# Long convolution by FFT and soft mixture of experts on one core: narrower first-stage products, a last stage packed into row groups, and an in-place spectral product

## The chip, the cores and the metric

The kernel runs on one core of a Trainium2 chip. The metric is the device time in microseconds of one execution, lower is better; the time given is the median of three runs. The engines are called by the profile's names: PE (matrix products; PEld is its weight load), DVE and POOL (elementwise), ACT (elementwise, and the copies out of PSUM), SP (issues nearly all transfers). PSUM is the memory that PE writes; it has eight banks of 128 x 512 floats.

## The reference

```python
def _attn_ref(x, h):                 # x: (8, 5696, 128), h: (5696, 128)
    Xf = np.fft.rfft(x, n=2 * S, axis=1); Hf = np.fft.rfft(h, n=2 * S, axis=0)
    return np.fft.irfft(Xf * Hf[None], n=2 * S, axis=1)[:, :S, :]

def _moe_ref(x, phi, w1, w2):        # x: (45568, 128), phi: (128, 32), 8 experts, 4 slots each
    logits = x @ phi
    d = exp(logits - logits.max(0)); d /= d.sum(0) + 1e-9
    slot_input = (d.T @ x).reshape(E, S_per_e, D)
    slot_out[e] = np.maximum(slot_input[e] @ w1[e], 0.0) @ w2[e]
    c = exp(logits - logits.max(1)); c /= c.sum(1) + 1e-9
    return c @ slot_out
```

Every channel of eight sequences is convolved with a filter of the same length. The result, seen as 45568 tokens, goes through a soft mixture of experts: one softmax over all tokens (dispatch), one over the 32 slots (combine).

## The kernel before

All data is float32, and each matrix product shows as two MATMUL passes in the profile. The convolution is a transform of length 90 x 64 in two stages, written as matrix products, with a product of spectra between and two stages back. There are nine groups: the filter (g = 0) and the eight sequences. Between the stages the data goes through buffers in DRAM: `f` behind the first stage, `z` behind the third.

**Stage A** (first stage, 90 frequencies). `load_x` (L190) loads a chunk of four columns n2 and their four mirror columns: 89 rows of 2 KB runs, in two transfers of 80 and 9 partitions. `fold` (L201, on POOL) makes the sum (comp 0) or the difference (comp 1) of the two halves. `stage_a(c, comp)` multiplies it (L212) by two tables of 128 columns, ACT copies each bank out (L214), and two transfers of 45 partitions, in runs of 1 KB, store to `f` (L218). A group has eight chunks.

**Stage B** works on units of four pairs of frequencies, twelve to a group. `load_g` (L236) loads `gt` from `f`; `stage_b1` makes the second transform (L250) into the two-bank PSUM tile `bt`, multiplies it by the filter's spectrum (L270, DVE, two products `pr` and `pi` in SBUF) and adds (L279, DVE; in the steps below 27 and from 72 on one of the two adds is POOL's). For the filter's group the products are with `turn`, and the sums (L274) are Hr and Hi. `stage_b2` is the third transform (L294); ACT copies the result out (L299), and one transfer of 512 KB stores it to `z` (L302).

**Stage C** works on pairs T, four to a sequence. `load_pair` (L330) loads 64 and 26 partitions of 16 KB runs. `stage_c1` makes the last transform: four products of 90 frequencies (128 rows with zeros), each as two column halves (L349); ACT copies two of the banks to `y` (L358) and `om` (L362); `fold_out` (L354, L355, DVE) forms sums and differences with the other two; four operations on POOL (L368) mirror them. Then `stage_c2` transposes (L377), `stage_c3` makes the logits (L386), `stage_c4` transposes them (L415), takes the row maximum (L430, DVE) and subtracts it (L431, POOL), `stage_c5` transposes the exponentials (L438), `softmax` ends the combine weights (L451 on POOL), `dispatch` accumulates the slots (L462), `stage_c6` transposes the combine weights (L486) and stores them. At the end come the experts and the output products (L819).

The order is written out by hand in one loop over steps t, and each engine runs its instructions in that order. Each step below 72 has one chunk of stage A; units of stage B come one (odd t) or two (even t) to a step; from t = 27 on `stage_c1` runs in every odd step. So two steps make a cycle. The core of the step, shortened:

```python
stage_a(t, 0); fold(t + 1, 0)
dispatch(pair(3)); slot_b(1)                # even steps
after = stage_c1(T, rows)                   # odd steps; rows is stage_c4
stage_c2(pair(1)); stage_c6(pair(5))        # even steps
after()                                     # odd steps: fold_out of om, four L368
slot_b(2); load_pair(pair(-2)); load_x(t + 3); stage_c5(U)
stage_a(t, 1); fold(t + 1, 1)
stage_c3(pair(1)); slot_b(3)                # even steps
```

`slot_b` makes `stage_b1` of one unit and `stage_b2` of the unit before. Each `fold` has one buffer to a comp. The products of stages A and C take their PSUM banks in turn from a ring of four until the end of stage B, then of eight.

Of the kernel before, what the change touches and what calls it, by code (L numbers as in the profile page):

```python
# [10 lines left out]
F32 = mybir.dt.float32  # L11
AF = mybir.ActivationFunctionType
AL = mybir.AluOpType
# [4 lines left out]
def z_blocks(n):  # L18

    return [(0, 64, 32), (64, n - 64, 0)]  # L20


def transform_tables(S, N1, N2, CH, X0, F0, F1):

# [14 lines left out]
    s1 = np.stack([np.cos(a1), -np.sin(a1), -np.cos(a1)], 1)  # L41
    a0 = np.outer(alpha, np.arange(N1 // 2) + 0.5)
    i1 = np.stack([np.cos(a0), -np.sin(a0), -np.cos(a0)], 1)
    NP = N1 // 2
    part = s1
    s1 = np.zeros((P, 3, P))
    for a, p in enumerate((F0, F1)):
        s1[X0:X0 + R1, :, p:p + NP] = part[:, :, a * NP:(a + 1) * NP]
    part = i1[np.arange(N1).reshape(2, NP).T.reshape(-1)]
    i1 = np.zeros((P, 3, N2))  # L50
    for r, n, p in z_blocks(N1):
        i1[p:p + n, :, 0:NP] = part[r:r + n]
# [5 lines left out]
    back = np.arange(N2).reshape(2, HALF // CH, CH).transpose(1, 0, 2).reshape(-1)  # L58
# [5 lines left out]
    for a in range(2):  # L64
        wq[a] = w[a * NP:(a + 1) * NP].transpose(1, 0, 2)
        for q in range(NP):
            vq[q % 2, :, q // 2, a] = w[a * NP + q][back].T
            tn[q % 2, :, 0, q // 4, a, q // 2 % 2] = np.cos(turn[a * NP + q]) / N
            tn[q % 2, :, 1, q // 4, a, q // 2 % 2] = np.sin(turn[a * NP + q]) / N
    wq, vq, tn = [t.reshape(P, *t.shape[2:]) for t in (wq, vq, tn)]  # L70
    return [np.ascontiguousarray(t, dtype=np.float32) for t in (s1, i1, wq, vq, tn)]
# [3 lines left out]
def kernel(  # L75
# [42 lines left out]
    assert S == R1 * N2 and R1 == N1 - 1 and D == P and CH == Q == 4  # L118
    SPLIT = R1 // 16 * 16
    X0, F0, F1 = 20, 6, 82  # L120
    ctx.enter_context(tc.manual_schedule())

    t_s1, t_i1, t_w, t_v, t_turn = [
        nc.inline_tensor(t, f"tab_{n}").ap()
        for n, t in zip(("s1", "i1", "w", "v", "turn"), transform_tables(S, N1, N2, CH, X0, F0, F1))]
    fd = [nc.dram_tensor(f"f_{g}", (2, N2, NP, 2, D), F32, kind="Internal").ap() for g in range(B + 1)]
    zd = [nc.dram_tensor(f"z_{b}", (NP, 2 * N2, 2, D), F32, kind="Internal").ap() for b in range(B)]
# [8 lines left out]
    i1 = const.tile([P, 3, HP], F32, name="i1")  # L136
# [24 lines left out]
    s1 = apool.tile([P, 3, P], F32, name="s1", tag="s1", bufs=1)  # L161
# [12 lines left out]
    xf = [apool.tile([P, CH, D], F32, name=f"x{i}", tag=f"x{i}", bufs=1) for i in range(2)]  # L174
# [4 lines left out]
    def load_x(c):  # L179
        if c >= (B + 1) * NJ:  # L180
            return
        g, j = divmod(c, NJ)
        src = (h if g == 0 else x[g - 1]).rearrange("(a n) d -> a n d", n=N2)
        t_ = xcs[c % len(xcs)]
        gap = N2 - CH * (2 * j + 1)
        for r in (slice(0, SPLIT), slice(SPLIT, R1)):
            v = src[r, CH * j:CH * (j + 1), :]
            v = bass.AP(tensor=v.tensor, offset=v.offset,
                        ap=[v.ap[0], [gap * D, 2], [1, CH * D]])
            nc.sync.dma_start(  # L190
                out=t_[X0 + r.start:X0 + r.stop, :, :, :].rearrange("p s n d -> p s (n d)"), in_=v)
        xs[c] = t_
# [3 lines left out]
    def fold(c, comp):  # L196
# [3 lines left out]
        y_ = xf[comp]  # L200
        nc.gpsimd.tensor_tensor(out=y_[:, :, :], in0=t_[:, 0, :, :], in1=t_[:, 1, ::-1, :],  # L201
                                op=AL.subtract if comp else AL.add)
        folded[(c, comp)] = y_

    def stage_a(c, comp):
        g, j = divmod(c, NJ)
        src = folded.pop((c, comp))
        tab = (0, 1) if comp == 0 else (1, 2)
        st = apool.tile([P, CH, 2, D], F32, name="fst", tag="fst", bufs=5)
        for G in range(2):  # L210
            p = bank()
            nc.tensor.matmul(p[:, :], s1[:, tab[G], :],  # L212
                             src[:, :, :].rearrange("p n d -> p (n d)"), start=True, stop=True)
            nc.scalar.activation(st[:, :, G, :],  # L214
                                 p[:, :].rearrange("p (n d) -> p n d", d=D), AF.Copy)
        n0 = comp * HALF + CH * j
        for a, p in enumerate((F0, F1)):
            nc.sync.dma_start(  # L218
                out=fd[g][a, n0:n0 + CH, :, :, :].rearrange("n q c d -> q n (c d)"),
                in_=st[p:p + NP, :, :, :].rearrange("k n c d -> k n (c d)"))  # L220
# [9 lines left out]
    def load_g(u):  # L230
        if u >= (B + 1) * NW:
# [5 lines left out]
            out=t_[:, 0:n, :, :].rearrange("p q c d -> p (q c d)"),  # L237
            in_=fd[g].rearrange("a r q c d -> (a r) (q c d)")[:, 8 * w * D:(8 * w + 2 * n) * D])
        gs[u] = t_

    def stage_b1(u, share):
# [15 lines left out]
        else:  # L257
            pv = bt[r, :, 0, :].rearrange("p a (c d) -> p a c d", c=2)
        k = 2 * m
        tags = ("yf", "yf") if g == 0 and w % 2 else ("pr", "pi")  # L260
        pr, pi = [bpool.tile([P, 4, 2, D], F32, name="p", tag=x, bufs=2 if x == "yf" else 1)
                  for x in tags]
        for p_, H_ in ((pr, turn[:, 0]), (pi, turn[:, 1])) if g == 0 else ((pr, Hr), (pi, Hi)):
# [6 lines left out]
            nc.vector.tensor_tensor(out=p_[r, 0:k, :, :], in0=pv, in1=h_, op=AL.mult)  # L270
        if g == 0:
            for c, op_, H_, eng in ((0, AL.add, Hr, nc.vector), (1, AL.subtract, Hi, nc.gpsimd)):
                h_ = H_[r, w, :, :, :].rearrange("p a o d -> p (a o) d") if m == 2 else H_[r, w, :, 0, :]
                eng.tensor_tensor(out=h_, in0=pr[r, 0:k, c, :], in1=pi[r, 0:k, 1 - c, :], op=op_)  # L274
            return
        y_ = bpool.tile([P, 4, 2, D], F32, name="yf", tag="yf", bufs=2)
        for c, op_, eng in ((1, AL.add, nc.gpsimd if share else nc.vector),
                            (0, AL.subtract, nc.vector)):
            eng.tensor_tensor(out=y_[r, 0:k, c, :], in0=pr[r, 0:k, c, :],  # L279
                              in1=pi[r, 0:k, 1 - c, :], op=op_)  # L280
        prods[u] = y_

    def stage_b2(u):
# [6 lines left out]
        for o, (i, n) in enumerate(us):  # L290
# [11 lines left out]
        nc.sync.dma_start(  # L302
            out=zd[g - 1][4 * w:4 * w + k, :, :, :].rearrange("q r c d -> r q (c d)"),
            in_=st[:, :, :, :].rearrange("p o q x -> p (o q) x")[:, 0:k, :])
# [4 lines left out]
    zn = used = None  # L309
    ybufs = [ypool.tile([P, Q * CH, D + 1], F32, name=f"y{i}") for i in range(2)]  # L310
    zring = [ypool.tile([P, 2, 2, CH, 2, D], F32, name="zc")]
# [4 lines left out]
    nc.vector.memset(zring[0][:, :, :, :, :, :], 0.0)  # L316
# [5 lines left out]
    def load_pair(T):  # L322
# [5 lines left out]
        w_ = 2 * 2 * CH * 2 * D  # L328
        for r, n, p in z_blocks(N1):
            nc.sync.dma_start(  # L330
                out=t_[p:p + n, :, :, :, :, :].rearrange("k h o n c d -> k (h o n c d)"),
                in_=zd[b].rearrange("q (a r) c d -> (q a) (r c d)",
                                    a=2)[r:r + n, j * w_:(j + 1) * w_])
        zs[T] = t_

    def stage_c1(T, between):
        t_ = zs.pop(T)
        kr = used if t_ is zn else P
# [7 lines left out]
        def product(o, tab, q):  # L346
            p = bank()
            for h_ in range(2):
                nc.tensor.matmul(p[h_ * HP:(h_ + 1) * HP, :], i1[0:kr, tab, :],  # L349
                                 t_[0:kr, h_, o, :, q, :], start=True, stop=True)  # L350
            return p[:, :].rearrange("p (n d) -> p n d", d=D)

# [4 lines left out]
        b_, a_ = product(0, 1, 1), product(0, 0, 0)  # L357
        nc.scalar.activation(part(0, 0), b_, AF.Copy)  # L358
        fold_out(a_, part(0, 0), part(1, 0))
# [506 lines left out]
```

## Time and profile before

| | |
|---|---|
| median of three runs | 924.53 us (923.91 to 933.71) |
| span of the profiled execution | 922.1 us; the page gives no other time for it |
| PE, PEld | 818.0 us (89%), 423.9 us (46%) |
| DVE, ACT, POOL | 653.1 us (71%), 481.7 us (52%), 488.1 us (53%) |
| moved by DMA | 272.45 MB, mean 295 GB/s, 156552 packets |
| largest groups | L212 on PE 275.9 us, L201 on POOL 192.8 us, L214 on ACT 171.9 us |
| f stores, gt loads, z stores, z loads | 288, 108, 96 and 64 transfers |

The page describes one profiled execution. "Busy" is the time in which an engine ran instructions of its own; matmuls are pipelined, so a busy PE need not be at its peak. The line of tenths shows the busy share in 40 equal slices of the span. In a timeline each line is a run of like instructions: start, length, engine, source line, operation, output and input, count, and in brackets the idle time before it and what ended it. SPq is SP's queue.

### The profile page before, as it was taken

To read this page: it belongs to the slowest core of one execution; us is meant where nothing else is said; L and a number is where in the kernel's file an instruction comes from. 1 tells how busy PE (TensorE), PEld (TensorE's weight loads), DVE (VectorE), ACT (ScalarE), POOL (GpSimd) and SP (SyncE) were. 2 spreads that over 40 slices of the span, in tenths; PEclk is the share of its full clock that TensorE was granted. 3 is DMA by queue.
4 is the path that set the end of the run, shared out by engine and by line. 5 is a ranking of instruction groups with operands and counts; after the bars stand their busy time and mean duration, and the time that the engine had idled before them with its cause. 6 is when DMAs were issued, how large, how long until landed. Compare 5 with 4: busy or idle time off the path is not lost.

```text
span 922.1 us, 19325 instructions
## 1 busy us (share of the span) xinstructions
PE 818.0 (89%) x7220; PEld 423.9 (46%) x7220; DVE 653.1 (71%) x887; ACT 481.7 (52%) x888; POOL 488.1 (53%) x426
## 2 busy tenths in 40 slices
PE   6968898899999999999999999999987777878893
PEld 2323344345444445544554454444444434345783
DVE  3047665478888878888888788988887775674552
ACT  4623454455556655555666666656553344475442
POOL 4648766546655565556565655655466552472000
PEclk9989999899999999999999999999999888798865
DMA  9989999999899999999999999999989887761798
GB/s 298 279 274 299 272 345 311 289 345 327 268 320 319 314 282 324 316 314 285 341 304 327 289 324 329 297 318 320 316 269 330 272 254 198 211 249 73 272 405 341
DMA packets 156552, 272.45 MB, mean 295 GB/s; under 512 B 11766, under 2 KB 114422, under 8 KB 153317
## 3 DMA queue, kind: packets, MB, share of 16 engines
q1 hardware_dynamic: 155883, 270.85, 91.4%
q8 instruction: 58, 0.95, 0.4%
q10 hardware_dynamic: 576, 0.36, 0.2%
q14 instruction: 35, 0.29, 0.1%
HBM read 142.86 MB, written 128.21 MB: 294 GB/s over the span
## 4 chain that ended last, share of the span: by engine, by line
PE 51%; DMA 31%; POOL 5%; DVE 5%; issue 3%; SPq 2%; ACT 2%; DVEq 0%; POOLq 0%; ACTq 0%
PE bank L212 17%; DMA zc<-z 11%; PE bank L349 9%; DMA gt<-f 8%; PE bt L250 7%; PE bz L294 6%; DMA out_dram<-o 4%; PE bank L377 4%; DVE p L270 2%; POOL y L368 2%; DMA f<-fst 2%; PE bank L462 2%; DMA z<-zst 2%; PE bank L438 2%; PE bank L386 2%
## 5 line engine op out<-in xcount | busy, mean ns | idle before, releaser
L212 PE MATMUL bank<-x,s 128*128 128x512 f32 x576 | 275.9, 614 | 12.3 <-POOL x L201 12.0
L201 POOL TENSOR_TENSOR x<-xc 128x512 f32<-128x512 f32 x144 | 192.8, 1342 | 154.7 <-PE bank L212 70.4
L214 ACT ACTIVATE fst<-bank 128x512 f32<-128x512 f32 x288 | 171.9, 597 | 95.5 <-PE bank L212 74.8
L299 ACT ACTIVATE zst<-bz 128x1024 f32<-128x1024 f32 x96 | 93.2, 971 | 205.4 <-PE bz L294 198.5
L270 DVE TENSOR_TENSOR p<-bt,Hr 128x1024 f32<-128x1024 f32 x96 | 112.9, 1176 | 108.0 <-PE bt L250 95.7
L212 PEld LDWEIGHTS bank<-x,s 128*128 128x128 f32 x576 | 102.4, 193 | 131.5 <-issue 93.4
L279 DVE TENSOR_TENSOR yf<-p 128x512 f32<-128x512 f32 (+1 forms) x163 | 146.4, 931 | 3.3
L250 PE MATMUL bt<-gt,wt 64*64 64x256 f32 x1620 | 116.4, 394 | 25.1 <-DMA gt<-f 22.0
L349 PE MATMUL bank<-zc,i 128*64 128x512 f32 x480 | 117.1, 610 | 7.0 <-DMA zc<-z 4.1
L294 PE MATMUL bz<-yf,vt 64*64 64x256 f32 x1440 | 104.9, 393 | 15.5 <-POOL yf L279 15.0
L270 DVE TENSOR_TENSOR p<-bt,Hi 128x1024 f32<-128x1024 f32 x96 | 112.3, 1170 | 0.0
L250 PEld LDWEIGHTS bt<-gt,wt 64*64 64x64 f32 x1620 | 55.0, 134 | 102.0 <-issue 31.6
L368 POOL TENSOR_TENSOR y<-y,op 128x512 f32<-128x512 f32 x64 | 77.5, 1211 | 7.8 <-DVE op L354 5.1
L294 PEld LDWEIGHTS bz<-yf,vt 64*64 64x64 f32 x1440 | 58.2, 137 | 44.2 <-POOL yf L279 21.0
L279 POOL TENSOR_TENSOR yf<-p 128x512 f32<-128x512 f32 (+1 forms) x29 | 45.9, 1583 | 53.9 <-DVE p L270 53.9
L368 POOL TENSOR_TENSOR y<-y,om 128x512 f32<-128x512 f32 x54 | 71.8, 1330 | 2.1
L270 DVE TENSOR_TENSOR p<-bt,turn 128x1024 f32<-128x1024 f32 (+1 forms) x24 | 27.2, 1174 | 57.8 <-PE bt L250 57.7
L349 PEld LDWEIGHTS bank<-zc,i 128*64 128x64 f32 x480 | 30.8, 138 | 68.3 <-issue 40.8
L377 PE MATMUL bank<-ident,y 109*128 109x109 f32 x512 | 60.0, 275 | 0.7 <-DVE y L368 0.7
L377 PEld LDWEIGHTS bank<-ident,y 109*128 109x128 f32 x512 | 53.5, 151 | 13.6 <-issue 11.9
L379 ACT ACTIVATE yt<-bank 128x360 f32<-128x360 f32 x128 | 50.9, 482 | 3.3 <-PE bank L377 3.3
L819 PE MATMUL op<-so,cT 32*128 32x128 f32 x704 | 46.0, 374 | 4.4 <-ACT o L828 3.6
(97 smaller groups left out, 851.5 us busy)
## 6 DMA issues: line engine op xcount, KB each, us to landing
f<-fst SPq DMA_DIRECT2D x288, 180.0 KB
gt<-f SPq DMA_DIRECT2D x99, 512.0 KB
z<-zst SPq DMA_DIRECT2D x88, 512.0 KB
zc<-z SPq DMA_DIRECT2D x30, 1024.0 KB
xc<-in_x_dram SPq DMA_DIRECT2D x64, 320.0 KB
out_dram<-o SPq DMA_DIRECT2D x16, 1024.0 KB
zc<-z SPq DMA_DIRECT2D x30, 416.0 KB
out_dram<-o SPq DMA_DIRECT2D x8, 768.0 KB
```

What stands on the lines that cost most here:

```text
L201: nc.gpsimd.tensor_tensor(out=y_[:, :, :], in0=t_[:, 0, :, :], in1=t_[:, 1, ::-1, :], op=AL.subtract if comp else AL.add)
L212: nc.tensor.matmul(p[:, :], s1[:, tab[G], :], src[:, :, :].rearrange("p n d -> p (n d)"), start=True, stop=True)
L214: nc.scalar.activation(st[:, :, G, :], p[:, :].rearrange("p (n d) -> p n d", d=D), AF.Copy)
L250: nc.tensor.matmul(bt[q * HP:(q + 1) * HP, a, o, :], wt[r, 2 * i + q, :], t_[r, 2 * o + q, :, :].rearrange("p c d -> p (c d)"), start=True ...
L270: nc.vector.tensor_tensor(out=p_[r, 0:k, :, :], in0=pv, in1=h_, op=AL.mult)
L279: eng.tensor_tensor(out=y_[r, 0:k, c, :], in0=pr[r, 0:k, c, :], in1=pi[r, 0:k, 1 - c, :], op=op_)
L294: nc.tensor.matmul(bz[a * HP:(a + 1) * HP, q, o, :], vt[r, i, a, :], y_[r, a * m + o, :, :].rearrange("p c d -> p (c d)"), start=True, sto ...
L299: nc.scalar.activation(st[:, 0:m, 0:n, :].rearrange("p o q x -> p q o x"), bz[:, 0:n, 0:m, :], AF.Copy)
L349: nc.tensor.matmul(p[h_ * HP:(h_ + 1) * HP, :], i1[0:kr, tab, :], t_[0:kr, h_, o, :, q, :], start=True, stop=True)
L368: eng.tensor_tensor(out=part_, in0=part(v, 0), in1=o_[:, :, :], op=sign)
L377: nc.tensor.transpose(p[:, i * TR:(i + 1) * TR], ys[T][0:TR, k * CH + i, 0:D], ident[0:TR, 0:TR])
L379: nc.scalar.activation(yt[:, k * CH:(k + 1) * CH, :, :], of_tokens(p), AF.Copy)
```

## The change

Tables and layouts change with the stages; what is computed stays.

- Stage A: the 90 frequencies are split into columns of 60 and 30. `stage_a(t, False)` makes the 60 of a chunk from both comps at once, two products of 64 columns side by side in one bank. `stage_a(t, True)`, in odd steps, makes the 30 of the last two chunks, four products of 32 columns side by side. Each stored run is 4 KB. The two folds of a chunk have one of three buffers of their own. The last nine rows of x go to partitions 100, 103, ... 124.
- Stage B: `gt` is loaded in runs of 1 KB. `pi` is made first; the other product overwrites `bt` in PSUM, and the adds read `bt` and `pi`. All adds are DVE's.
- `z` is stored by part of n2, in four transfers of 32 partitions (frequencies below 64), or eight (the last four units). C1's loads take two transfers of 128 partitions. Rows of the second buffer that no store fills are set to zero once, by eight transfers on ACT's queue.
- C1: 64 frequencies of both parts side by side in two row groups, and the other 26 in four row groups of 32, accumulated in the same four banks, which are all taken before `stage_c4`.

```diff
-        y_ = xf[comp]
+        y_ = xf[c % len(xf)]
...
-    def stage_a(c, comp):
+    def stage_a(c, high):
...
+        if high:
+            groups = [(c_, o, HALF, slice(HP, HP + HALF)) for c_ in (c - 1, c) for o in range(2)]
+        else:
+            groups = [(c, o, HP, slice(0, HP)) for o in range(2)]
+        for q in range(2):
             p = bank()
-            nc.tensor.matmul(p[:, :], s1[:, tab[G], :],
-                             src[:, :, :].rearrange("p n d -> p (n d)"), start=True, stop=True)
+            for i, (c_, o, m, cols) in enumerate(groups):
+                nc.tensor.matmul(p[i * m:(i + 1) * m, :], s1[:, q + o, cols], columns(c_, o),
+                                 start=True, stop=True)
...
-        for p_, H_ in ((pr, turn[:, 0]), (pi, turn[:, 1])) if g == 0 else ((pr, Hr), (pi, Hi)):
+        for p_, H_ in (((pi[r, 0:k, :, :], turn[:, 1]), (pv, turn[:, 0])) if g == 0 else
+                       ((pi[r, 0:k, :, :], Hi), (pv, Hr))):
...
-        for c, op_, eng in ((1, AL.add, nc.gpsimd if share else nc.vector),
-                            (0, AL.subtract, nc.vector)):
-            eng.tensor_tensor(out=y_[r, 0:k, c, :], in0=pr[r, 0:k, c, :],
-                              in1=pi[r, 0:k, 1 - c, :], op=op_)
+        for c, op_ in ((1, AL.add), (0, AL.subtract)):
+            nc.vector.tensor_tensor(out=y_[r, 0:k, c, :], in0=pv[:, :, c, :],
+                                    in1=pi[r, 0:k, 1 - c, :], op=op_)
...
-        b_, a_ = product(0, 1, 1), product(0, 0, 0)
-        nc.scalar.activation(part(0, 0), b_, AF.Copy)
-        fold_out(a_, part(0, 0), part(1, 0))
+        ps = {(o, c): bank() for o, c in ((0, 1), (1, 0), (0, 0), (1, 1))}
+        for c in (1, 0):
+            for h_ in range(2):
+                for o in range(2):
+                    r = slice(o * HP, (o + 1) * HP)
+                    nc.tensor.matmul(ps[o, c][h_ * HP:(h_ + 1) * HP, :], im[r, c, :],
+                                     zt[r, h_, :, c, :], start=True, stop=False)
+        for h_ in range(2):
+            for (o, c), p in ps.items():
+                r = slice((2 * o + c) * HALF, (2 * o + c) * HALF + N1 - MAIN)
+                nc.tensor.matmul(p[h_ * HP:(h_ + 1) * HP, :], ir[r, :], zx[r, h_, :, :],
+                                 start=False, stop=True)
+        nc.scalar.activation(part(0, 0), ps[0, 1], AF.Copy)
+        nc.scalar.activation(om[:, :, :], ps[1, 0], AF.Copy)
+        fold_out(ps[0, 0], part(0, 0), part(1, 0))
+        a_ = ps[1, 1]
         between()
-        b_, a_ = product(1, 1, 0), product(1, 2, 1)
-        nc.scalar.activation(om[:, :, :], b_, AF.Copy)
...
         if t < NA:
-            stage_a(t, 0)
+            stage_a(t, False)
             fold(t + 1, 0)
...
         if t < NA:
-            stage_a(t, 1)
+            if t % 2:
+                stage_a(t, True)
             fold(t + 1, 1)
```

## The prediction

> **What bounds the kernel now.** I read the page first, then stretches of the span, then one cycle of the middle in the order of time, then the waits and the chain that ended last.
>
> ```profile
> PE 818.0 (89%) x7220; PEld 423.9 (46%) x7220; DVE 653.1 (71%) x887; ACT 481.7 (52%) x888; POOL 488.1 (53%) x426
> DMA  9989999999899999999999999999989887761798
> ```
>
> TensorE and the DMA engines are both near full. By stretches, from the first product of stage C1 (182.60) to the last that still has stage A after it (664.70):
>
> ```profile
> 182.60:664.70 482.10, 469.80 (x4146) 234.99 (x4145) 407.14 (x542) 286.70 (x521) 277.02 (x240) 1.00 0.99 313
> ```
>
> The columns are the length, busy PE, PEld, DVE, ACT, POOL, granted clock, DMA share, GB/s. These 482.1 us hold 22 cycles of two steps, 21.91 us each, PE busy 21.35 of them, POOL only 12.6. So PE's order sets the pace and DMA just keeps up. One cycle, from stage A of an odd step on:
>
> ```profile
> 466.11 1.98 PE L212 MATMUL bank<-x,s 128*128 128x512 f32 x4
> ...
> 468.13 0.60 ACT L214 ACTIVATE fst<-bank 128x512 f32<-128x512 f32 x1 [0.26 <-PE bank L212]
> ...
> 468.72 1.94 PE L349 MATMUL bank<-zc,i 128*64 128x512 f32 x8 [0.62 <-ACT fst L214]
> ...
> 470.58 0.66 PE L415 MATMUL bank<-ident,lt 128*128 128x128 f32 x4
> ...
> 471.28 0.60 ACT L419 ACTIVATE L<-bank 128x512 f32<-128x512 f32 x1 [0.85 <-PE bank L415]
> ...
> 472.24 0.68 DVE L430 TENSOR_REDUCE rm<-L 128x16 f32<-128x512 f32 x1
> ...
> 472.36 0.60 ACT L362 ACTIVATE om<-bank 128x512 f32<-128x512 f32 x1
> ...
> 473.04 1.09 PE L250 MATMUL bt<-gt,wt 64*64 64x256 f32 x16
> 473.06 1.05 POOL L431 TENSOR_TENSOR L<-L,rm 128x512 f32<-128x512 f32 x1 [0.47 <-DVE rm L430]
> 473.23 0.69 DVE L354 TENSOR_TENSOR op<-bank,om 128x512 f32<-128x512 f32 x1 [0.31 <-PE bank L349]
> ...
> 474.07 2.44 POOL L368 TENSOR_TENSOR y<-y,op 128x512 f32<-128x512 f32 x2
> ...
> 475.42 3.60 PE L212 MATMUL bank<-x,s 128*128 128x512 f32 x8
> ...
> 476.48 2.76 POOL L368 TENSOR_TENSOR y<-y,om 128x512 f32<-128x512 f32 x2
> ...
> 478.95 1.09 PE L462 MATMUL bank<-y,d 128*32 128x129 f32 x32
> 479.20 1.71 POOL L201 TENSOR_TENSOR x<-xc 128x512 f32<-128x512 f32 x1
> ...
> 483.89 1.95 PE L212 MATMUL bank<-x,s 128*128 128x512 f32 x4
> ```
>
> The reader should follow POOL: after C1 it runs L431, four L368, and only then the second fold (L201) of the next chunk, ready at 480.91. PE began that chunk's first half (the last four of the eight L212) near 477.1 and needs the second fold only at 483.89. So the fold has 3 us to spare today, 3.8 us after the chunk's stage A began.
>
> **The change, part by part.** A matmul is two passes, one per 0.43 us for 512 columns (3.60 for eight); two side by side (L349) take eight passes in 1.94, four side by side (L250, 256 columns) sixteen in 1.09, so packing loses almost nothing.
>
> Stage A: four full products a chunk (3.44 us) become four of 64 columns, two side by side (1.72), and per two chunks eight of 32 columns, four side by side (1.72): 2.58 a chunk, 1.7 us less PE in a cycle. One eviction in four goes: 72 x 0.60 = 43 us of ACT, which is hidden (ACT is at 52%). C1: sixteen passes of 64 rows, four together (1.72), and sixteen of 26 rows, eight together (0.86; 1.72 if only four): 2.58 for 3.44. PE's own work so falls by 2.6 us a cycle.
>
> But stage A's first matmul pair now takes the even and the odd fold together, at the top of the step. In the even step that fold is the one that POOL makes after the four L368. This is a new wait, and behind it on PE stand the dispatch, two units of stage B, C2, C6, C3, stage A of the odd step, and the next C1, which feeds POOL. It closes a loop, and I add it up from E, the end of stage A in the odd step.
>
> C1 now takes four banks at once, and its second matmul needs the bank that stage A has just filled: the eviction ends 0.9 after E (L214: 0.26 wait and 0.60). Then 2.58: 3.45 with the first pass done early. Copy of the first bank 0.65: 4.1. The copy of om 0.60 and the transposes of L415 0.66 run together: 4.75; eviction of L 0.60: 5.35; rm 0.68: 6.05. Op on DVE 0.69: 6.75, while POOL's L431 takes 1.05: 7.15. Four L368 at 1.22: 12.05. Fold 1.27: 13.3. PE has meanwhile done L415, one unit each of B1 and B2, C5, the 32-column products and one 64-column product, and stands from about 9.7, so it idles 3.6 us. The rest of stage A, 1.7: 15.0. From the end of stage A to the next L212 (478.95 to 483.89) PE spends 4.94: 19.95. C3 waits for C2's evictions, 0.55, and takes 0.75; the next unit 1.8; stage A 1.7: 24.75.
>
> So a cycle is 24.75 instead of 21.91: 22 x 2.84 = +62. Low end: no 0.9 wait for the bank, 24.0, +46. High end: the rest of C1 only four side by side (+0.85), and the slow rows of L368 and L201 above (2.76 and 1.71: +0.75), 26.35, +98.
>
> In-place product: the second product is written to PSUM, of which no row exists. Nearest are L270 (1.22, PSUM to SBUF) and twice that. I take 1.22; the adds read PSUM and SBUF, as L354 does at 0.69, in place of L279's 0.98. DVE has 19.0 busy in 22.3 and loses none of its reserve. The bank pair is held 1.4 longer, but the next unit comes 5 us later; without that gap it would cost 1.4 a unit.
>
> DMA: the f stores become runs of 4 KB and the gt loads runs of 1 KB; by the trace's packet records (46 ns for one of 1 KB, 159 for 4 KB) one saves about what the other costs. The z stores go from 96 to 512. Each issue takes 0.32 us at least (L302), so 416 x 0.32 = 133 us more on SP, 4 us of each cycle. SP is issuing 14.5 us in the cycle shown; 18.5 fits into 24.75. The z loads now cover 128 partitions each, for 64 and 26.
>
> A rule of the Trainium skill speaks against this part: "DMA: Bandwidth & Descriptors" (Rules for kernel authors) wants many small transfers joined. With the fixed 2.0 us of that page (Anatomy of one DMA, for another kind of queue) and eight in flight, an estimate from it is 416 x 2.0 / 8 = 104 us, and the sum below would be 1071. The row has 0.32 us of issue, which lies beside the POOL loop, and the sum goes by that.
>
> The idle 3.6 us also touches the clock. In 160 to 168.8 us, where PE was busy 5.72 of 8.80, the granted clock was 0.81; in the middle, where gaps are short, 1.00. The Trainium skill, "TensorE: Matmul & The Clock Gate" (Part 1), halves the clock after a whole idle window of about 3.4 us; an estimate by it is that a gap of 3.6 us covers a window in one cycle of twenty, +2 us in all, and a gap of 5 us in half of them. No row here shows gaps of this size in the middle, and I add nothing.
>
> Before 182.6: PE loses 27 x 0.86 = 23 us of work, but gt loads and x loads end the waits there, and more stores and eight transfers of zeros come in. I take -1; from -12 (the share of L212 in the chain there, a quarter of it) to +10 (half of some 60 extra issues). From 664.7 to 769 the chain shows POOL's share of the yf sums:
>
> ```profile
> 692.90 1.23 POOL yf L279
> 694.17 1.67 PE bz L294 x16
> ```
>
> That goes to DVE. The cycle there is 20.8; DVE's own 17.6 (three units of 2 x 1.22 + 2 x 0.69, and 6.2 of the stages C) and 5.7 MB at about 300 GB/s (19) remain. 5 x 2 = -10, from -16 to 0. The tail waits twice for z loads:
>
> ```profile
> 773.48 11.15 DMA zc<-z
> ```
>
> Spread over all partitions, without the copy of the gap ahead, I take 3.5 off each (11.15 and 10.77) and 1 for C1: -8, from -14 to 0.
>
> **Sum.** +62 - 1 - 10 - 8 = +43 on the span of 922.1, 965. The median of the runs stands 2.4 above the span, so 967.5 us. What a measurement can tell here from no change is about 1%, 9 us.
>
> **Rivals.** Hidden wait: the saving of PE shows after all. Its place is the same loop, E to fold. It decides if the fold is ready by 11.3 instead of 13.3, as a cycle of 22.8 is then paid for by the 19 saved elsewhere; if it ends at DMA's floor, 21.0, the time is 22 x -0.9 - 19 = -39, 885. For it: POOL is at 53%, and its L368 might run faster when DVE no longer adds SBUF to SBUF. Against: five operations in a row, none under 1.05.
>
> SP's queue: its 34 issues a cycle, at the 0.63 mean of the cycle shown (14.5 for 23), are 21.4, and with 5 us of waits that are left, 27 a cycle: +112 - 19, 1018. For it: "SPq L236 <- DMA zc<-z" is 57.7 us of waits, in the instruction order each transfer waits for one of eight counters, used in turn. Against: small stores fill the rings less and issue in 0.32.
>
> No effect: the loop and the gains elsewhere cancel, within 1%.
>
> **Numbers.** Loop at 24 to 26: 0.72, whose own range is 945 to 995. SP's queue 0.10. Hidden wait 0.11. No effect 0.07. Range 938 to 1000: it leaves out the hidden wait and the far end of SP. Faster by over 1% 0.11, within 0.07, slower 0.82.
>
> **What would show it.** Right: the cycle of C1 near 24.75; PE waiting for POOL at stage A, some 3.6 us in each even step, among the longest waits; POOL without its 70.4 us of waits for PE at the fold; GB/s in the middle down to about 280; L212's sum a quarter smaller; yf adds at 0.69. Wrong: cycles of 22 or less, with DMA or gt loads ending PE's waits, or SP issuing without a pause.

## The result, and the profile after

The changed kernel takes 1033.88 us (median of four runs, 1029.09 to 1039.99), beside 929.12 for the kernel before on the same chip: a ratio of 1.113, with a 95% interval of 1.105 to 1.122. The profiled execution has a span of 1031.0 us for 922.1, 108.9 longer. The prediction was 967.5, with a range to 1000.

The page has these lines (busy time of PE, busy tenths of the DMA engines and granted clock in 40 slices):

```profile
PE 793.0 (77%) x8308; PEld 387.0 (38%) x8308; DVE 630.8 (61%) x928; ACT 440.7 (43%) x816; POOL 401.0 (39%) x385
PEclk9889889889989998999999989998999999897855
DMA  8789899799978987898799879877987899664499
```

No engine is full any more, and neither are the DMA engines. The same stretch as in the prediction, from the first product of C1 to the last that still has stage A after it, with the columns length, PE, PEld, DVE, ACT, POOL, granted clock, DMA share and GB/s:

```profile
205.70:783.20 577.50, 469.35 (x4852) 213.39 (x4850) 366.44 (x540) 262.78 (x476) 256.52 (x239) 0.94 0.87 270
```

Its 22 cycles take 26.25 us each for 21.91. So the 108.9 us are three pieces: 23.1 ahead of the first C1 (205.7 for 182.6), 22 x 4.34 = 95.4 in the middle, and 9.6 less behind it (247.8 for 257.4). PE lists 469 us of work in the middle, as before, although it has less of it; the clock, 0.94 for 1.00, accounts for some 35 us of that. One cycle in the order of time, from C1 on:

```profile
520.59 1.95 PE L375 MATMUL bank<-zc,im 64*64 64x512 f32 x16
522.47 1.11 PE L380 MATMUL bank<-zx,ir 26*64 26x512 f32 x16
...
526.28 0.68 DVE L367 TENSOR_TENSOR op<-bank,om 128x512 f32<-128x512 f32 x1
...
526.54 1.05 POOL L456 TENSOR_TENSOR L<-L,rm 128x512 f32<-128x512 f32 x1 [0.24 <-DVE rm L455]
...
527.55 2.45 POOL L393 TENSOR_TENSOR y<-y,op 128x512 f32<-128x512 f32 x2
...
529.96 2.44 POOL L393 TENSOR_TENSOR y<-y,om 128x512 f32<-128x512 f32 x2
...
532.35 1.26 POOL L199 TENSOR_TENSOR x<-xc 128x512 f32<-128x512 f32 x1
...
533.66 2.62 PE L217 MATMUL bank<-x,s 128*64 128x512 f32 x6 [3.39 <-POOL x L199]
536.21 1.95 PE L487 MATMUL bank<-y,d 128*32 128x129 f32 x32
```

Stage A of the odd step had ended at 520.6. The chain of the prediction is there link by link: C1, op on DVE, L456 (L431 before), four L393 (L368 before), the second fold (L199), and PE idle for 3.39 us until it. The fold is done 13.0 us after the end of stage A, for a predicted 13.3. The last two lines are slow: dispatch (L487) takes 1.95 us for the usual 1.09. From 534.8 to 538.2 the trace's clock record shows half clock. The list of waits of the middle names the pause:

```profile
PE bank L217 <- POOL x L199: 72.2, 21, 4.1
```

72.2 us in 21 waits, 3.4 us each, one in nearly every cycle. The in-place product costs what was predicted: the group of the second product shows 1.18 us (1.22 assumed), the sums 0.66 (0.69 assumed).

```profile
L279 DVE TENSOR_TENSOR bt<-bt,Hr 128x1024 f32<-128x1024 f32 x96 | 113.0, 1177 | 0.0
L287 DVE TENSOR_TENSOR yf<-bt,pi 128x512 f32<-128x512 f32 x192 | 119.3, 663 | 3.3
```

### The profile page after: what moved, and what is told of

The parts are those of the page before. It is cut to its first block, busy times and chain, and to the rows that moved or that the text cites. A ratio compares the mean times of both kernels' runs of the same rounds, so it can differ in the third digit from the quotient of the medians.

```text
span 1031.0 us, 21762 instructions
## 1 busy us (share of the span) xinstructions
PE 793.0 (77%) x8308; PEld 387.0 (38%) x8308; DVE 630.8 (61%) x928; ACT 440.7 (43%) x816; POOL 401.0 (39%) x385
## 4 chain that ended last, share of the span: by engine, by line
PE 41%; DMA 23%; POOL 12%; ACT 8%; issue 7%; SPq 5%; DVE 4%; POOLq 0%; DVEq 0%; ACTq 0%
PE bank L217 12%; DMA gt<-f 7%; POOL y L393 7%; PE bt L259 7%; PE bank L375 5%; PE bz L302 5%; DMA out_dram<-o 3%; ACT yt L404 3%; DMA f<-fst 3%; PE bank L487 3%; DMA xc<-in_x_dram 3%; PE bank L380 3%; ACT zst L307 2%; POOL x L199 2%; PE bank L411 2%
## 5 line engine op out<-in xcount | busy, mean ns | idle before, releaser
L217 PE MATMUL bank<-x,s 128*32 128x512 f32 (+1 forms) x1152 | 262.8, 657 | 89.4 <-POOL x L199 89.4
L199 POOL TENSOR_TENSOR x<-xc 128x512 f32<-128x512 f32 x144 | 180.4, 1269 | 237.7 <-DMA xc<-in_x_dram 95.6
L219 ACT ACTIVATE fst<-bank 128x512 f32<-128x512 f32 x216 | 128.9, 597 | 214.8 <-PE bank L217 185.5
L279 DVE TENSOR_TENSOR pi<-bt,Hi 128x1024 f32<-128x1024 f32 x96 | 112.9, 1176 | 98.3 <-PE bt L259 98.3
L217 PEld LDWEIGHTS bank<-x,s 128*32 128x32 f32 (+1 forms) x1152 | 60.4, 130 | 246.5 <-POOL x L199 118.0
L287 DVE TENSOR_TENSOR yf<-bt,pi 128x512 f32<-128x512 f32 x192 | 119.3, 663 | 3.3
L279 DVE TENSOR_TENSOR bt<-bt,Hr 128x1024 f32<-128x1024 f32 x96 | 113.0, 1177 | 0.0
L393 POOL TENSOR_TENSOR y<-y,op 128x512 f32<-128x512 f32 x64 | 77.5, 1211 | 5.2 <-DVE op L367 2.7
L393 POOL TENSOR_TENSOR y<-y,om 128x512 f32<-128x512 f32 x54 | 63.7, 1180 | 2.1
L375 PE MATMUL bank<-zc,im 64*64 64x512 f32 x480 | 60.2, 616 | 0.2 <-DMA zc<-zm 0.2
L279 DVE TENSOR_TENSOR pi<-bt,turn 128x1024 f32<-128x1024 f32 (+1 forms) x12 | 14.1, 1175 | 68.0 <-PE bt L259 68.0
L367 DVE TENSOR_TENSOR y<-bank,y 128x512 f32<-128x512 f32 x32 | 22.1, 692 | 48.6 <-ACT y L383 48.4
L383 ACT ACTIVATE y<-bank 128x512 f32<-128x512 f32 x32 | 19.1, 597 | 75.5 <-PE bank L380 75.5
```

What stands on the lines that cost most here:

```text
L199: nc.gpsimd.tensor_tensor(out=y_[:, comp, :, :], in0=t_[:, 0, :, :], in1=t_[:, 1, ::-1, :], op=AL.subtract if comp else AL.add)
L217: nc.tensor.matmul(p[i * m:(i + 1) * m, :], s1[:, q + o, cols], columns(c_, o), start=True, stop=True)
L219: nc.scalar.activation(st[:, :, q, :], p[:, :].rearrange("p (n d) -> p n d", d=D), AF.Copy)
L279: nc.vector.tensor_tensor(out=p_, in0=pv, in1=h_, op=AL.mult)
L287: nc.vector.tensor_tensor(out=y_[r, 0:k, c, :], in0=pv[:, :, c, :], in1=pi[r, 0:k, 1 - c, :], op=op_)
L375: nc.tensor.matmul(ps[o, c][h_ * HP:(h_ + 1) * HP, :], im[r, c, :], zt[r, h_, :, c, :], start=True, stop=False)
```

## The experiments

All times are medians with the kernel before (925 to 931 us) run on the same chip. "First C1" and "cycle" are read from C1's first products in each run's timeline; a cycle is the mean of the 22. The last column is the span from there on. These three columns are of the one profiled execution, which can lie several us off the median (with the old stage A it is the slowest of the four, 1009.7).

| kernel | time | ratio (95%) | first C1 | cycle | rest |
|---|---|---|---|---|---|
| before | 926.7 | | 182.6 | 21.91 | 257.4 |
| after | 1033.9 | 1.113 (1.105 to 1.122) | 205.7 | 26.25 | 247.8 |
| after, early fold | 1005.3 | 1.082 (1.077 to 1.087) | 205.3 | 24.78 | 250.0 |
| after, one z store a unit | 1029.5 | 1.110 (1.103 to 1.117) | 200.5 | 26.25 | 255.7 |
| after, both of these | 975.7 | 1.051 (1.044 to 1.058) | 198.0 | 23.52 | 257.5 |
| after, PE kept busy | 1015.8 | 1.091 (1.085 to 1.096) | 207.8 | 25.34 | 250.0 |
| after, old stage A | 1000.3 | 1.077 (1.071 to 1.084) | 204.7 | 25.03 | 252.5 |
| old stage A, one z store | 953.6 | 1.028 (1.024 to 1.033) | 195.7 | 23.23 | 252.2 |
| old stage A, two z stores | 978.2 | 1.057 (1.053 to 1.061) | 200.7 | 23.89 | 248.6 |
| before, z stores split by rows | 1026.5 | 1.108 (1.100 to 1.115) | 198.1 | 25.54 | 270.9 |
| before, new stage A, early fold | 943.3 | 1.019 (1.014 to 1.025) | 194.2 | 22.15 | 258.1 |

**Early fold.** The theory was the loop through POOL, with the halved clock on top; the rival was SP's queue.

```diff
             fold(t + 1, 0)
+            fold(t + 1, 1)
...
-            fold(t + 1, 1)
```

> Edit: the second fold of the next chunk is issued on POOL directly behind the first, ahead of C1's four L393. Theory (a loop through POOL: stage A's first pair waits for a fold that stands behind four L393, and the idle PE then runs at half clock): the wait for x at L217 goes, the middle's granted clock is 1.00 again, and a cycle falls from 26.25 to what the DMA engines need, 0.86 x 26.25 = 22.6, or to 21.9 as before the change; 22 x 3.65 to 4.35 = 80 to 96 less, 938 to 954 us. Rival (SP's queue with its 512 z stores sets the cycle, and the wait for the fold only fills the time in which SP is late anyway): the cycle stays at 25 or more, 1005 to 1034 us, with PE waiting for gt or z loads in place of the fold.

1005.3 us. PE's wait for the fold (L217 for L199) falls from 89.4 to 17.9 us in the whole span, as the two pages show (after, then this run):

```profile
L217 PE MATMUL bank<-x,s 128*32 128x512 f32 (+1 forms) x1152 | 262.8, 657 | 89.4 <-POOL x L199 89.4
L217 PE MATMUL bank<-x,s 128*32 128x512 f32 (+1 forms) x1152 | 227.7, 651 | 17.9 <-POOL x L199 17.9
```

So the loop is gone, but only 28 us come back: neither account holds alone. The cycles are uneven, from 20.6 to 29.0, four of them (one batch) 100 us. Where a long one lies, from the instructions of SP's queue and two stretches of that time:

```profile
484.73 5.00 SPq L321 DMA_DIRECT2D zr<-zst  x8
...
491.44 5.22 SPq L321 DMA_DIRECT2D zr<-zst  x8
```

```profile
485.00:491.00 6.00, 6.00 (x64) 2.55 (x68) 4.06 (x8) 3.76 (x7) 1.28 (x2) 0.91 0.74 213
491.00:497.00 6.00, 5.50 (x80) 3.69 (x76) 3.88 (x5) 3.32 (x7) 3.06 (x3) 1.00 0.66 177
```

SP needs 5 us to issue the eight stores of one remainder unit, 512 KB in all, which is 105 GB/s; meanwhile the DMA engines are a quarter to a third idle. So a second limit lies close under the loop. The granted clock of this middle is 0.92, so other pauses of PE still bring half clock; how much of the 24.78 that is, no run separates.

**Old stage A.** Stage A, folds, f and gt loads from the kernel before; z part and products from the kernel after.

```diff
-            stage_a(t, False)
+            stage_a(t, 0)
...
-            if t % 2:
-                stage_a(t, True)
+            stage_a(t, 1)
```

> Edit: stage A, its folds, the layout of f and the loads of gt are those of the kernel before; the z layout, C1 in 64 and 26 rows, the in-place product and the 512 z stores are those of the kernel after. Theory (loop through POOL): the second fold is needed only by the second half of stage A again, 3.8 us later, so the loop's wait goes; PE has 1.7 us more work a cycle than after, and the cycle is 21 to 22.6: 935 to 960 us, the start still late by the z stores and zeros. Rival (the z part costs the time by SP's queue): nothing of the z part was undone, the cycle stays at 25 or more, over 1000 us.

1000.3 us, the rival's answer: with no loop the cycle is still 25.0.

**PE kept busy.** Three products that nobody reads fill the pause.

```diff
+        if t % 2 == 0 and LAG_C < t < NA:
+            p = bank()
+            for i in range(3):
+                nc.tensor.matmul(p[:, :], ident[:, :],
+                                 wt[:, 8 * i:8 * i + 8, :].rearrange("p q r -> p (q r)"),
+                                 start=True, stop=True)
         if t < NA:
             stage_a(t, False)
```

> Edit: in every even step of the steady part three more 128x512 products, whose result nobody reads, are put on PE ahead of stage A, where PE stands idle for some 3.4 us waiting for the fold. Theory (of the 26.25 us of a cycle 24.75 are the loop and 1.5 are stage A, B1 and dispatch running at half clock after the gap): the granted clock of the middle goes from 0.93 to near 1.00, the cycle to 24.8, 22 x 1.5 = 33 less, 1001 us. Rival (the clock is low for another reason, or the loop is bound elsewhere): the added 3 x 0.86 = 2.6 us a cycle bring nothing or lengthen the time, 1031 to 1060 us.

1015.8 us, with 2.6 us more work for PE in each cycle:

```profile
207.80:765.20 557.40, 503.02 (x4985) 229.94 (x4984) 366.51 (x539) 262.81 (x476) 256.93 (x239) 0.99 0.88 278
```

The clock is 0.99, and all cycles but one (30.1) lie between 24.6 and 25.3, with the first at 28.3. That is the loop of the prediction, 24.75, bare. The middle is 20 us shorter, of the 33 expected; the rest stays in those two long cycles and in the 0.25 by which the loop is longer than summed.

**Zeros later.** The eight transfers of zeros go from the start to steps 12 to 15.

```diff
-    for i in range(8):
+        if t in range(NJ + 4, NJ + 8):
+            for i in (2 * (t - NJ - 4), 2 * (t - NJ - 4) + 1):
```

> Edit: the eight transfers of zeros into the memory of the z remainder are issued from ACT's queue in steps 12 to 15, two a step, and no longer ahead of everything at the start. Theory (they hold ACT's queue from 5.2 to 11.2 us and the x loads beside them, and the first B1 starts 8 us late for that): the first B1 comes at 52 to 56 instead of 60.5, and 4 to 8 us of the 23 lost before the first C1 come back: 1024 to 1030 us. Rival (the start is late by the small stores of f and z alone): the first B1 stays at 60, the time within 2 us.

1035.8 us, ratio 1.112 (1.106 to 1.119), no different from the kernel after in time. The profiled execution has its first C1 at 202.5, 3 us earlier, with cycles of 26.1: at most a few us are in the zeros.

**z stores from ACT's queue, with the early fold.**

```diff
-                    nc.sync.dma_start(out=zm...
+                    nc.scalar.dma_start(out=zm...
```

> Edit: the second fold early as in the run before (1005 us), and all 512 z stores are issued from ACT's queue in place of SP's. New theory (two floors: the loop through POOL at 25.0 a cycle, and under it SP's queue, as an early fold, the old stage A and a warm TensorE all gave 100 us for the four cycles of a batch, with DMA engines at 0.66 to 0.74 where eight small z stores of a unit follow one another on SP at 0.5 us each): with 73 issues a batch on SP for 137, a batch falls to 84 to 88 us, as before the change; 5.5 x 12 to 16 = 66 to 88 less, and up to 15 at the start: 905 to 940 us. Rival (the small stores cost their time in the DMA engines or in landing, not in the queue): still 100 a batch, 990 to 1010 us. Third (ACT's evictions stand behind the stores and PE behind them): 950 to 990.

1172.3 us, ratio 1.267 (1.259 to 1.276), worse than all three expected. ACT's own order shows it:

```profile
444.05 4.41 ACTq L321 DMA_DIRECT2D zr<-zst  x8
448.51 0.60 ACT L466 ACTIVATE d<-bank 128x512 f32<-128x512 f32 x1 [4.49 <-DMA zr<-zst]
```

The eviction of d, for which PE's dispatch waits, stands 4.5 us behind eight stores. The third case was right in kind and far too small. The run says nothing on SP's queue.

**Two z stores a unit, with the early fold.** B2 writes its rows in the order part, parity, row, and a store takes both parities: 256 stores for 512, of the same packets.

```diff
-                    nc.tensor.matmul(bz[a * HP:(a + 1) * HP, q, o, :], vt[r, i, a, :],
+                    for e in range(2):
+                        nc.tensor.matmul(bz[e * HP + a * HALF:e * HP + (a + 1) * HALF, q, o, :],
+                                         vt[r, i, a, e * HALF:(e + 1) * HALF],
```

> Edit: the second fold early, and B2 writes its rows in the order part, parity, row (four products of 32 columns for two of 64), so that a z store takes both parities: 2 stores a unit for 4, and 4 for 8 in the remainder, 256 in all for 512, all on SP; packets, bytes and layout of z as after. Theory (SP's queue): 105 issues a batch for 137, 16 us less issuing of 70; a batch falls from 100 to 84 to 90: 915 to 955 us. Rival (packets of 512 bytes and 1 KB, not issues, cost the time): the packets are the same, 990 to 1010 us.

970.7 us, ratio 1.046 (1.038 to 1.055), cycle 23.6: 35 us for 256 issues.

**The kernel before with split z stores.** The cleanest test: four stores of 32 partitions for one, eight in the last units of a batch. Only the packets of these last units change as well, from 1 KB to 512 bytes.

```diff
-        nc.sync.dma_start(out=zd[g - 1][4 * w:4 * w + k, :, :, :]...
+        for i in range(4):
+            r = slice(i * HALF, (i + 1) * HALF)
+            if 8 * w < HP:
+                nc.sync.dma_start(out=zd[g - 1][4 * w:4 * w + k, r, :, :]...
+                continue
+            for c in range(2):
+                nc.sync.dma_start(out=zd[g - 1][4 * w:4 * w + k, r, c, :]...
```

> Edit to the kernel before, nothing else changed: each z store of 512 KB is split into four of 32 partitions, and from unit 8 of a batch on into eight, by the two parts of the complex number, so that there are 512 z stores of the sizes of the kernel after; the layout of z stays. Theory (SP's queue): 52 more issues in a batch of 88 us, 0.5 each, +26 us of SP's time against 26 us of pauses there: a batch comes to 95 to 102 and the start is later too, 980 to 1020 us. Rival (my prediction's step: the issues lie beside other work): 925 to 940 us.

1026.5 us: 100 us for splitting the stores, nearly as much as the whole change. The smaller packets are no rival: in the middle 16640 of 512 bytes at 31 ns, for half as many of 1 KB at 48 ns, are 7 us more for the 16 DMA engines, and the middle is 80 longer. The long cycles lie again where the units of eight are issued:

```profile
485.80 4.80 SPq L311 DMA_DIRECT2D z<-zst  x8
```

```profile
475.00:505.00 30.00, 21.28 (x186) 10.92 (x184) 18.57 (x25) 12.78 (x24) 12.32 (x11) 1.00 0.78 218
```

But these rows are not the whole cost. In the middle ten of them run without a break, 4.4 us each, with 206 GB/s; the time outside them has only 275 GB/s for the 313 of the kernel before. At 313 the bytes of the ten rows would take some 15 us less, and the middle is 80 longer. How the stores cost the rest was not taken apart.

**The same count in another cut**, by frequency, each store over all 128 partitions.

```diff
+        for i in range(k):
+            nc.sync.dma_start(out=zd[g - 1][4 * w + i, :, :, :]..., in_=sv[:, i, :])
```

> Edit to the kernel before, nothing else changed: each z store is split into four by frequency, each over all 128 partitions, and from unit 8 of a batch on into eight, by the complex part too: 464 z stores of the same sizes as those split by partitions (1027 us), of the same packets. Theory (number of issues on SP): 1005 to 1030 us as there. Rival (a store that covers 32 partitions is slower in landing than one over 128, as it reads few rows of the buffer): 930 to 970 us.

1009.1 us, ratio 1.084 (1.076 to 1.093), cycle 24.66. With 464 stores for 512 that is 82 for 100 us: the count sets most of the cost, and little is left for the number of partitions a store covers.

**The in-place product alone**, on the kernel before.

```diff
-                       ((pr, Hr), (pi, Hi)):
+                       ((pi[r, 0:k, :, :], Hi), (pv, Hr)):
```

> Edit to the kernel before, nothing else changed: the in-place product, with all sums on DVE. Theory (as in the prediction): product 1.22 to 1.18 in PSUM, sums 0.66 for 0.98; nothing in the middle, -10 (-16 to 0) after the last stage A: 908 to 930 us, likeliest 918. Rival (the bt bank is held 1.4 us longer, and without the idle time of the loop the next unit's B1 waits for it): 66 units in the middle at up to 1.4, 940 to 1010 us.

925.4 us, ratio 0.999 (0.994 to 1.003): the time shows neither the 10 us expected behind the middle nor the rival's waits.

**One z store a unit.** z in the order frequency, part, row, so that the 128 rows of a unit go out in one store (two in the remainder). First with loads that ask for both parts at once, so that their outermost count is 2; with the early fold and without:

```diff
-    zm = [nc.dram_tensor(f"zm_{b}", (2, MAIN, HALF, 2, D), F32, kind="Internal").ap() for b in range(B)]
+    zm = [nc.dram_tensor(f"zm_{b}", (MAIN, 2, HALF, 2, D), F32, kind="Internal").ap() for b in range(B)]
...
+            out=zm[g - 1][8 * w:8 * w + 2 * k].rearrange("(q a) o r c d -> (a o r) q (c d)", a=2),
+            in_=sv[:, 0:k, :])
```

> Edit: the second fold early, and z in an order of frequency, part, row (the remainder: complex part, frequency, part, row), so that a unit's z goes out in one store over all 128 partitions, in two in the remainder: 128 z stores in all for 512; packets keep their 1 KB and 512 bytes, C1 and its two z loads are as after. Theory (the number of stores on SP; half as many gave 971 for 1005): 89 issues a batch for 137, the batch at what the DMA engines need, 84 to 88 us; 895 to 930 us, likeliest 915. Rival (the packets of 512 bytes and the loop share the rest): 950 to 970.

> Edit: only the z order of the run before, with one and two stores a unit; the second fold stays behind C1's four L393 as in the kernel after. Theory of the loop (my prediction without SP's queue): PE waits for the fold in every even step, cycles of 24.75 to 26.25 as after, by the loop and the halved clock; the start is earlier by most of the 23 us: 990 to 1015 us. Rival (the wait for the fold was only where SP's lateness showed, and the z stores are the whole cost): cycles below 23, 915 to 950 us.

1702.6 and 1704.0 us (ratios 1.830 and 1.832). From the waits of the first:

```profile
PE bank L371 <- DMA zc<-zm: 386.5, 30, 18.1
```

The packets of such a load (8 KB, 309 ns each, 128 of them) come two at a time, some 20 us for 1 MB, while the DMA engines are at 0.46 in the middle. The Trainium skill, "DMA: Bandwidth & Descriptors" (Why a DMA increments its semaphore by 16 and not by 1), says that the largest number up to 16 that divides the slowest dimension of both patterns is the number of engines used, which for a count of 2 is what the packets show. Then with each load cut by part into two of 64 rows:

```diff
+        for o in range(2):
+            nc.sync.dma_start(out=t_[0][o * HP:(o + 1) * HP]..., in_=zm[b][:, o, j * n:(j + 1) * n]...
```

> Edit: second fold early and one z store a unit (two in the remainder), as in the run of 1703 us, but each z load is issued in two, one for each part of n2, so that its outermost count is 64 partitions and no longer 2. Theory (that run was slow because a load whose outermost count is 2 went out two packets at a time, some 20 us for 1 MB; the z stores' number is the cost in the kernel after): 97 issues a batch for 137, the batch at 84 to 90 us, 895 to 935 us. Rival (the wider stores themselves are slow): over 1000 us.

> Edit: the same z order and z loads by part; the second fold stays behind C1's four L393 as in the kernel after. Theory of the loop: PE waits for the fold in every even step, cycles of 24.75 to 26.25, the start earlier: 985 to 1015 us. Rival (the wait for the fold only filled the time in which SP was late): cycles below 23, 905 to 950 us.

975.7 and 1029.5 us: the four corners. The two middles:

```profile
198.00:715.50 517.50, 443.63 (x4850) 214.99 (x4848) 371.83 (x540) 260.63 (x476) 258.02 (x239) 0.94 0.99 294
```

```profile
200.50:778.10 577.60, 473.19 (x4850) 214.86 (x4848) 366.07 (x540) 262.87 (x476) 256.45 (x239) 0.93 0.92 269
```

With the loop (second line) the cycle is 26.25, to the second digit that of the kernel after: as long as the loop stands, 384 stores fewer are worth some 4 us, within the noise (the intervals of the two ratios overlap); in the profiled executions the start is 5 shorter and the end 8 longer. Without the loop the same 384 stores are worth 30 (1005.3 to 975.7). The runs with one store also cut each z load in two, so the 30 hold both; halving the stores with the loads as they were was worth 35. Without either the DMA engines are full, 0.99, which fits a cycle held at 23.5 by them.

**The last 48 us.** The f part alone on the kernel before, with the early fold, and the z part alone in the two ways of storing.

```diff
-            stage_a(t, 0)
+            stage_a(t, False)
+            fold(t + 1, 0)
+            fold(t + 1, 1)
```

> Edit to the kernel before: stage A in 60 and 30 columns with its x rows, the layout of f and the loads of gt in pieces of 1 KB, as in the kernel after, but with the second fold early; z, C1 and the products are those of before. Theory A (the last 45 us, which neither the loop nor the 512 stores explain, are the z part: loads and stores of z share the SBUF and the DMA engines worse, 294 GB/s for 313): no z part here, so 905 to 935 us. Theory B (they are the f part: 1 KB pieces of gt and 4 KB pieces of f): cycles of 23.5, 960 to 980 us.

> Edit to the kernel after: stage A, folds, f and gt loads of before; z with one store a unit (two in the remainder) and loads by part. Theory A (z part): still 23 to 23.5 a cycle, 955 to 980 us. Theory B (f part): 21.5 to 22 a cycle, 915 to 940 us.

> Edit to the kernel after: stage A, folds, f and gt loads of before; z with two stores a unit (four in the remainder), each over 64 partitions, and loads over 128 partitions as after. Theory A (z part, by 512-byte packets and 40 more issues a batch): 950 to 975 us. Theory B (f part): 920 to 945 us. If it is 25 or more below the run with one store and loads by part, the loads by part are what is dear in that one.

943.3, 953.6 and 978.2 us: 18 for the f part and 28 for the z part, which add up to the 48. Both theories have a share. In the f part 12 of the 18 come ahead of the first C1 and 5 from the middle. In the z part (old stage A, one z store) the DMA engines are full (1.00 in this stretch of the middle), and a cycle takes 23.23 us:

```profile
198.00:697.00 499.00, 460.56 (x4391) 236.99 (x4378) 360.22 (x530) 279.24 (x508) 253.25 (x236) 0.96 1.00 299
```

Two stores a unit with loads over 128 partitions are slower still with the old stage A (978), but level with one store and loads by part with the new one and the early fold (971 and 976); which of the two ways of loading z is dearer stays open.

No kernel here beat the kernel before; the in-place product alone equals it.

## Why the prediction was right and wrong

**Right: the sign, and the loop that sets it.** Fold at 13.0 for 13.3, idle 3.4 for 3.6, the cycle at full clock 25.0 for 24.75, PE's wait for POOL at stage A the longest wait of PE. Taking the fold forward or stage A back removes it. One sign of the prediction failed: L217's sum is 262.8 us for L212's 275.9, not a quarter smaller, as stage A is what runs behind the pause; with the new stage A on the kernel before (middle clock 1.00) it is 228.

**Where the 66 us went.** The span is 1031.0 for a sum of 965. The cycle is 1.5 longer than the 24.75, which is 33 in all; the start is 24 later than forecast, and the end gains 8 less.

**Wrong: the clock, "I add nothing".** The cycle is 26.25 for 25.0, and 22 x 1.25 = 28 us are lost; the middle's clock says about the same, 0.06 x 577.5 = 35. With the pause filled the clock is 0.99 and the middle 20 shorter. I had quoted the rule of the Trainium skill, "TensorE: Matmul & The Clock Gate" (Part 1), that a whole idle window of about 3.4 us halves the clock, and from it an estimate of one cycle in twenty. The clock record of the kernel after has 15 half-clock stretches in the middle, of 3.41 to 10.24 us and 72 in all, for 21 waits. Their starts are whole multiples of 3.413 us apart, so the record can be read window by window. Each of the 15 follows a window in which PE was busy for 0.4 to 1.40 us. After none of the 133 other windows at full clock does the clock fall, and PE was busy for more than that in all of them. With the early fold the border lies at 1.75. So here the window need not be wholly idle, and a pause of 3.4 us brought half clock in two cycles of three; the measurement decides.

The range had room for this in its own terms. Their high ends, +98 and +10 with nothing gained behind the middle, come to 1032, but the range stopped at 1000. That 26.25 lies so near the 26.35 of the high end is luck: that end stood for other causes, a rest of C1 at half the rate and slow L368, and neither came (L380 takes 1.11 us, two L393 2.45, L199 1.26).

**Wrong: the start, -1 for +23.** In the corners the z stores are 5 to 7 of it, the zeros about 3 in one profile; the f part alone shows 12, the z part with one store 13, both together 15. The step that failed is "half of some 60 extra issues" as the most that could go against it: SP issues 48 more there (257 for 209), about as I counted, but the f layout and the z layout delay the start as well, each by more than that bound, and I had charged them with nothing. The granted clock ahead of the first C1 is 0.88 for 0.96, so part of it may be half clock again. What in the layouts does it was not taken apart.

**Wrong: the end, -18 for -9.6.** The five cycles that still have stage B take 96.2 us for 103.1: -7.0, where the sums of yf were to give -10. The four steps from there to the last C1 take 40.4 for 45.9: -5.5, for -8; PE's waits for z loads, 7.6 us before, are down to under 2. And 2.9 are lost again in the experts' products, where the granted clock is 0.55 for 1.00 (the chain before, then after):

```profile
846.11 3.64 PE bank L764 x32
952.21 6.50 PE bank L790 x32
```

So both gains were taken too large and a second loss to the clock was left out. How much of the 7.0 the sums of yf gave is open: the in-place product alone left the time as it was.

**The z stores: right as priced, wrong as understood.** "Lies beside the loop" holds to some 4 us. But I priced an issue by its 0.32 us and compared SP's total with the length of a cycle. A part of the cost comes in bursts: the remainder units of a batch bring three times eight stores with little between them, and the DMA engines move 177 to 213 GB/s meanwhile for the 313 of the kernel before. That what is late then is not made up in a kernel whose DMA engines are full is argued, not shown. Alone the split costs 100 us on the kernel before. The rule of the Trainium skill, "DMA: Bandwidth & Descriptors" (Rules for kernel authors), that many small transfers should be joined, spoke against it, and the estimate from it (104 us) is near what the split stores cost alone. No run here shows the 2.0 us a transfer it was made of, so the agreement may be luck. On top of the loop, where I set it aside, they cost some 4, within the noise.

**The rivals.** The hidden wait (885) did not come about (L393 takes the 1.21 us of L368), and without the loop it would not have either: under the loop at 25.0 lay SP at 24.8 and the DMA engines at 23.5, all above 21.9. "It ends at DMA's floor, 21.0" was the wrong step: I let the f and z layouts cost the DMA engines nothing, from packets of 1 and 4 KB, and their floor rose to 23.5 (294 GB/s for 313; the 8 KB packets of the z loads take 535 ns in the mean of the middle when loaded by part, 369 in loads of 128 rows, 309 at best). SP's queue was priced at 27 a cycle; without the loop it is 24.8, and 25.5 on the kernel before with the stores split.

**What the 107 us are.** f part 18, z part 28 (sum 46; about 48 measured together); the loop with its clock 54 more (975.7 to 1029.5); the number of stores some 4 more, within the noise. Counted the other way, the stores come to 30 and the loop to 28. The parts overlap in time and have no price of their own.

## What to carry to other kernels

Before a saving is counted, list what sets the cycle next once the first limit goes, and the one after that: here they lay at 26.25, 24.8 and 23.5 us a cycle, so that removing the first, which seemed to cost 95 us, brought 28. Count the issues of a queue in the densest stretch, not over a cycle, and multiply their size by their rate to see whether the DMA engines are still fed. A new pause of PE of some 3 us can cost more than its length: here half clock followed two of three, and filling the pause gave 20 us back.

## What the runs showed of the hardware

A load whose outermost count is 2 moves on two DMA engines: 20 us for 1 MB, and 1703 us for the kernel. In the middle of the kernel after, half clock came in whole windows of 3.413 us on one grid, behind each full-clock window with up to 1.40 us of PE's work and behind none with more; with the early fold the border was 1.75, and in three further runs it lay between 1.4 and 1.9, not always as sharp. Eight stores on ACT's queue keep it from its next eviction for 4.5 us. In the kernel after a store of 128 KB takes 0.51 us in the mean to issue on SP, and one of the remainder (64 KB or less) 0.46; before, one of 512 KB takes 0.51. So the time hardly goes by the size, and the rows of eight shown, 512 KB in 4.8 to 5.2 us, feed the DMA engines with 100 to 109 GB/s.
